# Attention inputs laid out by the host with time along the row, and one scan with its reciprocal in place of two scans

## The chip, the cores and the metric

The kernel runs on one core of a Trainium2 chip. The metric is the device time of one execution in microseconds (us), as the median of several executions. A core has five engines that run side by side, each with its own queue: TensorE (PE in the profile; its weight loads are PEld), VectorE (DVE), ScalarE (ACT), GpSimd (POOL) and SyncE (SP), which here issues most of the transfers. They wait for one another by semaphores. SBUF is the on-chip memory of 128 partitions, PSUM the small memory that TensorE writes to. What the host does with numpy before the launch isn't part of the metric.

## The reference

Two parts follow each other: a linear attention with a decay for every key channel, and a mixture of eight experts of which each token takes one.

```python
batch, n_heads, seq, head_dim = (4, 8, 768, 48)
for t in range(S):
    state = alpha[:, :, t, :, None] * state + einsum('bhd,bhe->bhde', k[:, :, t], v[:, :, t])
    y[:, :, t] = einsum('bhd,bhde->bhe', q[:, :, t], state)
...
x = ascontiguousarray(y.transpose(0, 2, 1, 3)).reshape(B * S, H * D)     # 3072 x 384
logits = x @ w_gate + modality_bias[modality_id]
e_idx = argmax(logits, axis=1)
# probs: softmax of the logits, gate_w: that of the chosen expert
for e in range(8):
    h = maximum(x[mask] @ w1[e], 0.0)               # 384 -> 1024, mask: tokens of e
    out[mask] = gate_w[mask, None] * (h @ w2[e])    # 1024 -> 384
```

All inputs are float32; alpha lies between 0.8 and 1.0.

## The kernel before

**Tiles.** The 3072 tokens are cut into 24 tiles of 128 time steps (NU = 24), six for each batch element. A tile has eight heads of 48 channels; two heads share the 112 partitions of a tile with time along the row: one on partitions 0 to 47, the other on 64 to 111. So a tile of k, q or alpha with time along the row is 112 partitions by 4 pairs by 128 time steps.

**Decays.** Inside a tile the recurrence is turned into matrix products. A key is multiplied by the product of the decays on one side of its time step, a query by that on the other side, and then the scores are plain products of the scaled keys and queries, masked to the past. Before the change, `decay` runs a scan over alpha from the end of the tile to its start (G, L257), which gives each key the decay from its own step to the end. `decay_back` takes the reciprocal of the four whole-tile products (L265) and runs a second scan forward from it (Fw, L267), which gives each query its factor. Rows have segments of 129 columns (SEG): one for each of four pairs, with a column to start the scan anew.

**Inputs.** `load` (L130 to 135) brings alpha, k, q and v with time along the partitions, 48 channels (192 bytes) at a time. TensorE turns alpha, k and q by transposes against an identity matrix (`trans`, L243), four for each, 12 in a step. Alpha is copied from PSUM into X by ScalarE (`decay_in`, L252; in step 0 by VectorE); k and q are read by VectorE from PSUM as they are scaled (`scale_keys`, L283, and `scale`, L291).

**The loop.** L849 to 891 run 24 steps. Step s works on several tiles: the decays of tile s, the scaling, scores and masks of tile s-1, the outputs of tile s-2, the rows of x of tile s-3 (stored to a buffer in DRAM), and the routing of tiles done before. `natural` turns the scaled keys back (L297), `update` forms the tile's own contribution to the state and adds the decayed old one (L354 to 360), `state` and `outputs` form the rows of y (L329, L336). The order on TensorE, VectorE and ScalarE is that in which the code is written (`manual_schedule`, L847), so an instruction that waits holds up all that stand behind it on its engine; GpSimd's work is ordered by a planner. GpSimd masks the scores (L314), keeps the smallest decay product (`amin`, L260) and updates the state (S and T, L358 and L360). `guard` (L270) checks on ScalarE that no alpha is too large; in that case, or where a product got too small, a slow general path runs at the end.

**Routing.** After tiles 5, 11, 15, 19 and 23, `groups` starts the routing of a group: `route_flow` and for two of them `route_early` choose experts and count places, in pieces that `advance` puts into the following steps, with small matrix products on TensorE in between. Behind the loop (L893 to 952) the last tiles, the last routing group and the first expert's work are interleaved by hand. Then the experts run: seven more units of up to 512 tokens.

**Buffers.** Natural-layout tiles of a, k and q have NB = 4 buffers, v has 6; the loads run PF = 3 tiles ahead. PSUM tiles named "tr" (3) take the transposes, "sc" (2) the scores and, before the change, the routing's small products.

Of the kernel before, what the change touches and what calls it, by code (L numbers as in the profile page):

```python
# [21 lines left out]
P = 128  # L22
B, H, S, D = 4, 8, 768, 48
NC = S // P
NP = H // 2
SEG = P + 1
W = 64 + D
SEGS = NP * SEG + 12
DM = H * D
# [34 lines left out]
@with_exitstack  # L64
def attention_moe(ctx: ExitStack, tc: tile.TileContext, q, k, v, alpha, mid, wg, mb, w1, w2, out):
    nc = tc.nc
# [18 lines left out]
    NB, PF, NV = 4, 3, 6  # L85
    nat = {}
    ident = cp.tile([P, P], F32, name="ident")
    make_identity(nc, ident)
    for i in range(NB):
        for n, val in (("a", 1.0), ("k", 0.0), ("q", 0.0)):  # L90
            t = na.tile([P, H, 64], F32, name=f"nat_{n}{i}")
            nat[n, i] = t
            pool.memset(t[:, :, D:], val)

    VT = []
    for i in range(NV):
        t = ac.tile([P, H, 64], F32, name=f"vt{i}")
        VT.append(t)
        pool.memset(t[:, :, D:], 0.0)

# [28 lines left out]

    def load(i, names="akqv"):  # L130
        b, c = divmod(i, NC)
        for n, t in (("a", alpha), ("k", k), ("q", q), ("v", v)):
            if n in names:
                dst = VT[i % NV][:, :, :D] if n == "v" else nat[n, i % NB][:, :, :D]
                sp.dma_start(dst, t[b, :, c * P : (c + 1) * P, :].rearrange("h t d -> t h d"))

    wgs = cp.tile([P, ND, E], F32, name="wgs")
    for n in "a0 k0 q0 a1 v0 a2 k1 q1 v1 a3 k2 q2 v2".split():
        load(int(n[1]), n[0])
    still = ac.tile([P, 4 * P], BF16, name="still")  # L140
# [3 lines left out]
    def warm(n):  # L144
        for _ in range(n):
            pe.matmul(idle, still[:, :P], still, start=True, stop=True)

    warm(7)
    wgp = ac.tile([P, 2, 2, 32], F32, name="wgp")
# [4 lines left out]
    for c in range(2):  # L154
        for g in range(2):
# [3 lines left out]
            )  # L159
    DR = na.tile([W, SEGS], F32, name="DR")[:, : NP * SEG + 1]  # L160
    vec.memset(DR, AFLOOR)
    vec.memset(DR[:, SEG :: SEG], 1.0)
    X, DF, T1 = [], [], []
    for i in range(2):
        t = na.tile([W, SEGS], F32, name=f"X{i}")[:, : NP * SEG + 1]
        vec.memset(t[:, 0 :: SEG], 0.0)
        X.append(t)
        t = na.tile([W, SEGS], F32, name=f"DF{i}")[:, : NP * SEG]
        vec.memset(t, 0.0)
        DF.append(t)  # L170
    for i in range(3):
        t = ac.tile([W, NP, 64], F32, name=f"T1{i}")
        pool.memset(t[:, :, D:], 0.0)
        T1.append(t)
    na.tile([P, 8], F32, name="padr")
    bhi = ac.tile([P, 1], F32, name="bhi")
    vec.memset(bhi, -float(ALPHA_MAX_BITS))
    gacc = ac.tile([P, NU], F32, name="gacc")
    amin = ac.tile([W, NU, NP], F32, name="amin")
    junk = ac.tile([P, DM], F32, name="junk")  # L180
    L = cp.tile([P, NU, E], F32, name="L")
# [57 lines left out]

    def trans(i, n):  # L240
        p = ps.tile([W, NP, P], F32, name="tr", bufs=3)
        for j in range(NP):
            pe.transpose(  # L243
                p[:, j], nat[n, i % NB][:, 2 * j : 2 * j + 2].rearrange("p a b -> p (a b)")[:, :W], ident
            )
        if i == 0 or (i == 1 and n == "a"):
            warm(1)
        return p

    def decay_in(i):  # L250
        pa = trans(i, "a")
        (act.copy if i else vec.tensor_copy)(seg(X[i % 2][:, 1:], 0), pa)  # L252

    def decay(i):
        x = X[i % 2]
        G = na.tile([W, SEGS], F32, name="G", bufs=4)[:, : NP * SEG + 1]
        vec.tensor_tensor_scan(  # L257
            G[:, 1:][:, ::-1], x[:, 1:][:, ::-1], DR[:, 1:][:, ::-1], 0.0, op0=ALU.mult, op1=ALU.max
        )
        pool.tensor_copy(amin[:, i], G[:, 1::SEG])  # L260
        st[i, "G"] = G

    def decay_back(i):
        x, d, G = X[i % 2], DF[i % 2], st[i, "G"]
        vec.reciprocal(d[:, 0::SEG], G[:, 1::SEG])  # L265
        Fw = na.tile([W, SEGS], F32, name="Fw", bufs=3)[:, : NP * SEG]
        vec.tensor_tensor_scan(Fw, x[:, :-1], d, 0.0, op0=ALU.mult, op1=ALU.add)  # L267
        st[i, "F"] = Fw

    def guard(i):  # L270
        return act.activation(
            junk.rearrange("p (a b) -> p a b", b=D),
            nat["a", i % NB][:, :, :D].bitcast(U32),
            AF.Relu,
            bias=bhi,
            scale=1.0,
            accum_out=gacc[:, i : i + 1],
        )

    def scale_keys(i):  # L280
        kh = sb.tile([W, NP, P], F32, name="kh")
        pk = trans(i, "k")
        vec.tensor_tensor(kh, pk, seg(st[i, "G"][:, 1:], 1), op=ALU.mult)  # L283
        st[i, "k"] = kh

    def scale(i):
        if i:
            scale_keys(i)
        qh = sb.tile([W, NP, P], F32, name="qh", bufs=3)
        pq = trans(i, "q")  # L290
        vec.tensor_tensor(qh, pq, seg(st[i, "F"], 1), op=ALU.mult)  # L291
        st[i, "q"] = qh

# [53 lines left out]
    def update(i):  # L347
        if i % NC == NC - 1:
            return
        kn, vt = st[i, "n"], VT[i % NV]  # L350
        kv = ps.tile([W, NP, D], F32, name="kv")
        for h in range(H):
            r = slice(64 * (h % 2), min(64 * (h % 2) + 64, W))
            pe.matmul(kv[r, h // 2], kn[:, h // 2, r], vt[:, h, :D], start=True, stop=True)  # L354
        S1 = sb.tile([W, NP, D], F32, name="S")
        act.copy(S1, kv)
        if i % NC > 0:
            pool.tensor_tensor(S1, S1, T1[i % 3][:, :, :D], op=ALU.add)  # L358
        A = st[i + 1, "G"][:, 1::SEG].unsqueeze(2).broadcast_to([W, NP, D])
        pool.tensor_tensor(T1[(i + 1) % 3][:, :, :D], S1, A, op=ALU.mult)  # L360

# [74 lines left out]
    def route_flow(t0, t1):  # L436
# [16 lines left out]
        yield  # L453
        rp = ps.tile([P, n, E], F32, name="sc", bufs=2)
        pe.matmul(rp, tri, oh[:, s], start=True, stop=False)
# [76 lines left out]
    def route_early(s):  # L532

        n = EARLY[s]
        yield
        cnt = ps.tile([P, E], F32, name="sc", bufs=2)
        pe.matmul(cnt, ones, ohs, start=True, stop=(s == 0))
# [28 lines left out]
        yield  # L566
        tp = ps.tile([P, 2], F32, name="sc", bufs=2)
        for t in range(n):
# [131 lines left out]
    fl = cp.tile([P, 2], F32, name="fl")  # L700
    pool.memset(fl, 1.0)
    flb = cp.tile([P, 1], BF16, name="flb")
    fli = cp.tile([1, 1], I32, name="fli")

    def out_of_range():
        vec.tensor_reduce(fl[:, 0:1], gacc, axis=AX.X, op=ALU.max)
        vec.tensor_reduce(fl[:W, 1:2], amin.rearrange("p a b -> p (a b)"), axis=AX.X, op=ALU.min)
        vec.tensor_scalar(fl[:, 0:1], fl[:, 0:1], 0.0, None, op0=ALU.is_gt)
        vec.tensor_scalar(fl[:, 1:2], fl[:, 1:2], AMIN, None, op0=ALU.is_lt)
        vec.tensor_tensor(flb, fl[:, 0:1], fl[:, 1:2], op=ALU.add)  # L710
        yield
# [102 lines left out]
    def live(i):  # L814
        return 0 <= i < NU
# [33 lines left out]
    for s in range(NU):  # L849
        if s > 0 and s + PF < NU:  # L850
            load(s + PF, "a")
        if s > 0 and s + PF - 1 < NU:
            load(s + PF - 1, "kqv")
# [3 lines left out]
        if s != 1:
            decay_in(s)
        if live(s - 1):
            scale(s - 1)  # L860
        if s == 1:
            decay_in(s)
        if live(s - 3):
            rows(s - 3)
        if live(s - 4) and s % 2:
            logits_rows(s - 4)
        advance()
        if live(s - 1) and (s - 1) % NC < NC - 1:
            natural(s - 1)
        decay(s)  # L870
        if s == 0:
            scale_keys(s)
        if s < NU - 1:
            advance()
# [353 lines left out]


# [20 lines left out]
```

## Time and the profile before

| | us |
|---|---|
| median of three runs | 369.85 (369.78 to 370.48) |
| the profiled execution | 370.23 |
| its span, first to last instruction | 368.5 |
| attention steps, first scan to last scaled query | 6.0 to 137.6 |
| TensorE busy over the span | 356.3 (97%) |
| VectorE busy over the span | 218.3 (59%) |
| ScalarE | 188.1 (51%) |
| GpSimd | 155.6 (42%) |

The page gives a picture of the span in 40 equal slices, each a digit for tenths of busy time:

```profile
PE   8899999999999999999899999999999999999993
DVE  6887879788889875888565415522660456036400
ACT  2766777777767564347454325524451535164310
POOL 9945347426536663047337326313712471220021
PEclk9999999999999999999999999999999999999998
DMA  9999999989899995897756317333633473110011
GB/s 135 166 164 165 178 207 199 195 179 193 171 194 182 199 368 193 297 334 223 254 168 212 101 58 265 101 107 91 232 94 121 134 229 106 65 44 5 1 45 50
```

A slice is 9.2 us, so the attention fills the first 15. PEclk is the clock granted to TensorE, in tenths of the full one; DMA is the busy share of the 16 DMA engines. In the groups further down, a row has the line, engine, operation, what is written and read, the shapes, the count, then busy time in us, the mean duration in ns, and the idle time just before it with what ended it. In a view in order of time, a row begins with the start and the duration in us.

### The profile page before, as it was taken

How to read it: one execution, taken by the hardware profiler on the slowest of the kernel's cores; microseconds unless marked ns; L12 is line 12 of the kernel's file. 1: busy time of each engine (PE TensorE's matmuls, PEld its weight loads, DVE VectorE, ACT ScalarE, POOL GpSimd, SP SyncE). 2: the span in 40 equal slices, each digit the busy share in tenths (PEclk: the TensorE clock that was granted, in tenths of full speed). 3: DMA queues.
4: the chain of work that ended last, by engine and by line, in shares of the span. 5: the costliest groups of instructions: out<-in, count | busy, mean ns of one | idle time of the engine just before them, and what ended most of it. 6: DMA issues, size and time to landing. Idle time of an engine off the chain costs nothing. (4 is left out here: it accounts for less than half of the span.)

```text
span 368.5 us, 9337 instructions
## 1 busy us (share of the span) xinstructions
PE 356.3 (97%) x3666; PEld 314.5 (85%) x3666; DVE 218.3 (59%) x420; ACT 188.1 (51%) x367; POOL 155.6 (42%) x237
## 2 busy tenths in 40 slices
PE   8899999999999999999899999999999999999993
PEld 4788888888988787899888998899899988978992
DVE  6887879788889875888565415522660456036400
ACT  2766777777767564347454325524451535164310
POOL 9945347426536663047337326313712471220021
PEclk9999999999999999999999999999999999999998
DMA  9999999989899995897756317333633473110011
GB/s 135 166 164 165 178 207 199 195 179 193 171 194 182 199 368 193 297 334 223 254 168 212 101 58 265 101 107 91 232 94 121 134 229 106 65 44 5 1 45 50
DMA packets 122730, 59.18 MB, mean 161 GB/s; under 512 B 102857, under 2 KB 114168, under 8 KB 122676
## 3 DMA queue, kind: packets, MB, share of 16 engines
q1 hardware_dynamic: 118196, 48.78, 57.5%
q0 software_dynamic: 4032, 9.68, 7.9%
q8 instruction: 31, 0.51, 0.6%
q14 instruction: 23, 0.19, 0.2%
q10 hardware_dynamic: 448, 0.01, 0.1%
HBM read 49.01 MB, written 9.50 MB: 159 GB/s over the span
## 5 line engine op out<-in xcount | busy, mean ns | idle before, releaser
L965 POOL DMA_INDIRECT out_dram<-os,odx x23 | 23.5, 1020 | 104.4 <-ACT os L1033 93.1
L999 PE MATMUL sc<-w2H,hH 128*128 128x384 f32 x192 | 65.1, 339 | 0.0
L1001 PE MATMUL sc<-w2H,hL 128*128 128x384 f32 x192 | 64.2, 334 | 0.0
L1000 PE MATMUL sc<-w2L,hH 128*128 128x384 f32 x192 | 64.2, 334 | 0.0
L836 DVE TENSOR_TENSOR w1L<-w1r,w1H 128x768 fp32r<-128x768 f32 x24 | 22.0, 955 | 63.1 <-ACT w1H L834 57.7
L1018 PE MATMUL tr<-xH,w1H 128*128 128x512 f32 (+1 forms) x144 | 53.8, 374 | 0.0
L1020 PE MATMUL tr<-xH,w1L 128*128 128x512 f32 (+1 forms) x144 | 53.5, 372 | 0.0
L1019 PE MATMUL tr<-xL,w1H 128*128 128x512 f32 (+1 forms) x144 | 53.5, 371 | 0.0
L828 DVE SCALAR_TENSOR_TENSOR hL<-tr,hH 128x512 fp32r<-128x512 f32 x47 | 32.3, 688 | 32.8 <-ACT hH L826 25.6
L826 ACT ACTIVATE hH<-tr 128x512 fp32r<-128x512 f32 x47 | 28.0, 598 | 44.9 <-PE tr L1020 24.5
L314 POOL TENSOR_SCALAR_AFFINE_SELECT scT<-scT 128x512 f32<-128x512 f32 x48 | 38.0, 815 | 21.5 <-ACT scT L313 21.5
L1033 ACT ACTIVATE os<-sc,gg 128x384 f32<-128x384 f32 x23 | 13.4, 582 | 64.8 <-PE sc L1001 37.3
L696 POOL DMA_INDIRECT gg<-gd,idx x25 | 26.9, 1076 | 25.8 <-DMA gd<-gs 18.8
L999 PEld LDWEIGHTS sc<-w2H,hH 128*128 128x128 f32 x192 | 36.1, 188 | 1.1 <-issue 1.0
L1000 PEld LDWEIGHTS sc<-w2L,hH 128*128 128x128 f32 x192 | 36.1, 188 | 0.1
L1001 PEld LDWEIGHTS sc<-w2H,hL 128*128 128x128 f32 x192 | 36.0, 188 | 0.0
L313 ACT COPY scT<-sc 128x512 f32<-128x512 f32 x48 | 25.8, 589 | 14.5 <-PE sc L309 14.4
L267 DVE TENSOR_TENSOR_SCAN Fw<-X,DF 112x516 f32<-112x516 f32 x24 | 32.0, 1335 | 0.8
L690 POOL DMA_INDIRECT xg<-xd,idx x25 | 26.6, 1063 | 11.5 <-issue 4.9
L1020 PEld LDWEIGHTS tr<-xH,w1L 128*128 128x128 f32 x144 | 27.1, 188 | 4.7
L1018 PEld LDWEIGHTS tr<-xH,w1H 128*128 128x128 f32 x144 | 27.1, 188 | 4.6
L1019 PEld LDWEIGHTS tr<-xL,w1H 128*128 128x128 f32 x144 | 27.1, 188 | 4.6
(245 smaller groups left out, 672.9 us busy)
## 6 DMA issues: line engine op xcount, KB each, us to landing
w1r<-in_moe_w_dram SPq DMA_DIRECT2D x16, 768.0 KB
w2r<-in_moe_w_dram SPq DMA_DIRECT2D x16, 768.0 KB
nat_a<-in_alpha_dram SPq DMA_DIRECT2D x24, 192.0 KB
nat_k<-in_k_dram SPq DMA_DIRECT2D x24, 192.0 KB
nat_q<-in_q_dram SPq DMA_DIRECT2D x24, 192.0 KB
vt<-in_v_dram SPq DMA_DIRECT2D x24, 192.0 KB
xd<-xs SPq DMA_DIRECT2D x24, 192.0 KB
xg<-xd,idx POOLq DMA_INDIRECT x25
```

The source lines that it names most:

```text
L267: vec.tensor_tensor_scan(Fw, x[:, :-1], d, 0.0, op0=ALU.mult, op1=ALU.add)
L314: pool.affine_select(s, s, [[0, NP], [1, P]], ALU.is_ge, 0.0, base=0, channel_multiplier=-1)
L690: pool.indirect_dma_start(xg[x][:, u], None, xd[0:rows], IOA(idx[:, c : c + 1], 0), bounds_check=rows - 1, oob_is_err=False)
L696: pool.indirect_dma_start(gg[x][:, u : u + 1], None, gd[0:rows], IOA(idx[:, c : c + 1], 0), bounds_check=rows - 1, oob_is_err=False)
L826: act.activation(hH, hp, AF.Relu)
L828: vec.scalar_tensor_tensor(hL, hp, 0.0, hH.bitcast(F32), op0=ALU.max, op1=ALU.subtract)
L999: pe.matmul(op, hH[:, us] if f is None else hH[:, f, us], wH, start=first, stop=False)
L1000: pe.matmul(op, hH[:, us] if f is None else hH[:, f, us], wL, start=False, stop=False)
L1001: pe.matmul(op, hL[:, us] if f is None else hL[:, f, us], wH, start=False, stop=final)
L1018: pe.matmul(hp, wH[:, d, fs], XH[:, d, :n], start=(d == 0), stop=False)
L1019: pe.matmul(hp, wH[:, d, fs], XL[:, d, :n], start=False, stop=False)
L1020: pe.matmul(hp, wL[:, d, fs], XH[:, d, :n], start=False, stop=(d == ND - 1))
```

## The change

The host lays out two new inputs. `turned` holds for each of the 24 tiles 112 partitions by 1552 columns: keys (512), queries (512), and alpha in four segments of 129, each behind a column with 0 (ones and zeros fill partitions 48 to 63). `rowsv` holds v with time along the partitions, each head padded to 64 columns. The general path still reads q, k, v and alpha as they are.

On the chip the transposes of alpha, k and q go, with X, DF and the copy into X. One forward scan G gives the product of the decays since the tile's start, restarted by the 0 and a 1.0 in DR at the head of each segment; R is the reciprocal of all 516 columns of G. Keys are multiplied by R, queries by G; the state's decay is G's last column of the same tile. `scale(s)` runs in step s, after the first `advance`, no longer in step s+1, and `groups` stands behind it. The guard reads alpha in the new layout. The routing's small products use the PSUM tiles "tr" in the loop and "sc" behind it. The first four loads bring all 112 partitions, later ones the 96 with data. Four more warm-up products of TensorE stand at the start.

```diff
+AW = NP * SEG + 12
+KW = NP * P
+RW = 2 * KW + AW
...
+    TN = [na.tile([W, RW], F32, name=f"tn{i}") for i in range(NB)]
...
+    def load(i, v=True):
+        if i >= NB:
+            for r in (slice(0, D), slice(64, W)):
+                sp.dma_start(TN[i % NB][r], turned[i, r])
+        elif i:
+            sp.dma_start(TN[i], turned[i])
+        else:
+            for c in (slice(2 * KW, RW), slice(0, KW), slice(KW, 2 * KW)):
+                sp.dma_start(TN[0][:, c], turned[0, :, c])
+        sp.dma_start(VT[i % NV], rowsv[i])
...
-    warm(7)
+    warm(11)
...
+    DR = na.tile([W, AW], F32, name="DR")[:, : NP * SEG]
     vec.memset(DR, AFLOOR)
+    vec.memset(DR[:, 0::SEG], 1.0)
...
     def decay(i):
-        x = X[i % 2]
...
-    def decay_back(i):
...
+        G = na.tile([W, AW], F32, name="G", bufs=3)[:, : NP * SEG]
+        vec.tensor_tensor_scan(G, TN[i % NB][:, 2 * KW : 2 * KW + NP * SEG], DR, 0.0, op0=ALU.mult, op1=ALU.max)
+        pool.tensor_copy(amin[:, i], G[:, P::SEG])
+        R = na.tile([W, AW], F32, name="R", bufs=2)[:, : NP * SEG]
+        vec.reciprocal(R, G)
+        st[i, "G"], st[i, "R"] = G, R
...
     def scale(i):
+        for n, z, f in (("k", 0, "R"), ("q", 1, "G")):
+            t = sb.tile([W, NP, P], F32, name=n + "h", bufs=3)
+            src = TN[i % NB][:, z * KW : (z + 1) * KW].rearrange("p (a b) -> p a b", b=P)
+            vec.tensor_tensor(t, src, seg(st[i, f], 1), op=ALU.mult)
+            st[i, n] = t
...
-        A = st[i + 1, "G"][:, 1::SEG].unsqueeze(2).broadcast_to([W, NP, D])
+        A = st[i, "G"][:, P::SEG].unsqueeze(2).broadcast_to([W, NP, D])
...
-        rp = ps.tile([P, n, E], F32, name="sc", bufs=2)
+        rp = ps.tile([P, n, E], F32, **place)
...
     for s in range(NU):
+        if s + PF < NU:
+            load(s + PF)
...
+        decay(s)
+        if live(s - 1) and (s - 1) % NC < NC - 1:
+            natural(s - 1)
         if live(s - 3):
             rows(s - 3)
         if live(s - 4) and s % 2:
             logits_rows(s - 4)
         advance()
-        if live(s - 1) and (s - 1) % NC < NC - 1:
-            natural(s - 1)
-        decay(s)
-        if s == 0:
-            scale_keys(s)
+        scale(s)
         if s < NU - 1:
             advance()
         if s % 2:
             groups(s - 4)
-        decay_back(s)
-        guard(s)
...
+        guard(s)
         if live(s - 2):
             state(s - 2)
         if live(s - 1):
             scores(s - 1)
...
     L0 = NU - 1
-    scale(L0)
+    place.update(name="sc", bufs=2)
     rows(L0 - 2)
```

More of the change, by code (lines that the diff above doesn't have):

```diff
@@ L27 @@
 W = 64 + D
-SEGS = NP * SEG + 12
+AW = NP * SEG + 12
+KW = NP * P
+RW = 2 * KW + AW
 DM = H * D
@@ L64, in attention_moe @@
 @with_exitstack
-def attention_moe(ctx: ExitStack, tc: tile.TileContext, q, k, v, alpha, mid, wg, mb, w1, w2, out):
+def attention_moe(ctx: ExitStack, tc: tile.TileContext, q, k, v, alpha, mid, wg, mb, w1, w2, turned, rowsv, out):
     nc = tc.nc
@@ L85, in attention_moe @@
     NB, PF, NV = 4, 3, 6
-    nat = {}
     ident = cp.tile([P, P], F32, name="ident")
     make_identity(nc, ident)
[L89 to L93, printed above, removed]
+    TN = [na.tile([W, RW], F32, name=f"tn{i}") for i in range(NB)]
     VT = []
@@ L98, in attention_moe @@
         VT.append(t)
-        pool.memset(t[:, :, D:], 0.0)
     WR = [
@@ L128, in first_unit @@
             )
[L130 to L135, printed above, removed]
+    def load(i, v=True):
[8 more added lines that the diff above has]
+        sp.dma_start(VT[i % NV], rowsv[i])
     wgs = cp.tile([P, ND, E], F32, name="wgs")
-    for n in "a0 k0 q0 a1 v0 a2 k1 q1 v1 a3 k2 q2 v2".split():
-        load(int(n[1]), n[0])
+    for i in range(PF):
+        load(i)
     still = ac.tile([P, 4 * P], BF16, name="still")
@@ L159, in attention_moe @@
             )
-    DR = na.tile([W, SEGS], F32, name="DR")[:, : NP * SEG + 1]
+    DR = na.tile([W, AW], F32, name="DR")[:, : NP * SEG]
     vec.memset(DR, AFLOOR)
[L162 to L170, printed above, removed]
+    vec.memset(DR[:, 0::SEG], 1.0)
+    na.tile([P, 8], F32, name="padr")
+    T1 = []
     for i in range(3):
@@ L174, in attention_moe @@
         T1.append(t)
-    na.tile([P, 8], F32, name="padr")
     bhi = ac.tile([P, 1], F32, name="bhi")
     vec.memset(bhi, -float(ALPHA_MAX_BITS))
-    gacc = ac.tile([P, NU], F32, name="gacc")
+    gacc = ac.tile([W, NU], F32, name="gacc")
     amin = ac.tile([W, NU, NP], F32, name="amin")
-    junk = ac.tile([P, DM], F32, name="junk")
+    junk = ac.tile([W, NP * SEG], F32, name="junk")
     L = cp.tile([P, NU, E], F32, name="L")
@@ L238, in seg @@
         return t.rearrange("p (a b) -> p a b", b=SEG)[:, :, lo : lo + P]
[L240 to L252, printed above, removed]
-    def decay(i):
-        x = X[i % 2]
[L256 to L261, printed above, removed]
-    def decay_back(i):
[L264 to L268, printed above, removed]
+    def decay(i):
+        G = na.tile([W, AW], F32, name="G", bufs=3)[:, : NP * SEG]
[4 more added lines that the diff above has]
+        st[i, "G"], st[i, "R"] = G, R
     def guard(i):
         return act.activation(
-            junk.rearrange("p (a b) -> p a b", b=D),
-            nat["a", i % NB][:, :, :D].bitcast(U32),
+            junk,
+            TN[i % NB][:, 2 * KW : 2 * KW + NP * SEG].bitcast(U32),
             AF.Relu,
-            bias=bhi,
+            bias=bhi[:W],
             scale=1.0,
@@ L278, in guard @@
         )
[L280 to L284, printed above, removed]
-    def scale(i):
[L287 to L292, printed above, removed]
+    def scale(i):
+        for n, z, f in (("k", 0, "R"), ("q", 1, "G")):
[3 more added lines that the diff above has]
+            st[i, n] = t
     def natural(i):
@@ L427, in attention_moe @@
     odx = cp.tile([P, NH], I32, name="odx")
+    place = {"name": "tr", "bufs": 3}
     def route_begin():
@@ L535, in route_early @@
         yield
-        cnt = ps.tile([P, E], F32, name="sc", bufs=2)
+        cnt = ps.tile([P, E], F32, **place)
         pe.matmul(cnt, ones, ohs, start=True, stop=(s == 0))
@@ L566, in route_early @@
         yield
-        tp = ps.tile([P, 2], F32, name="sc", bufs=2)
+        tp = ps.tile([P, 2], F32, **place)
         for t in range(n):
@@ L700, in attention_moe @@
     fl = cp.tile([P, 2], F32, name="fl")
-    pool.memset(fl, 1.0)
+    pool.memset(fl[:, 0:1], 0.0)
+    pool.memset(fl[:, 1:2], 1.0)
     flb = cp.tile([P, 1], BF16, name="flb")
@@ L705, in out_of_range @@
     def out_of_range():
-        vec.tensor_reduce(fl[:, 0:1], gacc, axis=AX.X, op=ALU.max)
+        vec.tensor_reduce(fl[:W, 0:1], gacc, axis=AX.X, op=ALU.max)
         vec.tensor_reduce(fl[:W, 1:2], amin.rearrange("p a b -> p (a b)"), axis=AX.X, op=ALU.min)
@@ L849, in attention_moe @@
     for s in range(NU):
[L850 to L853, printed above, removed]
+        if s + PF < NU:
+            load(s + PF)
         if s == 4:
@@ L856, in attention_moe @@
             sp.dma_start(gd[MID : MID + 1], zr[:, 0:1])
[L857 to L862, printed above, removed]
+        decay(s)
+        if live(s - 1) and (s - 1) % NC < NC - 1:
+            natural(s - 1)
         if live(s - 3):
@@ L1227, with laid_out @@
 _OUTS = [((N, DM), "float32")]
+def laid_out(np, q, k, v, alpha):
+    turned = np.zeros((NU, W, RW), np.float32)
+    for z, x in enumerate((k, q)):
+        x = x.reshape(B, NP, 2, NC, P, D).transpose(0, 3, 2, 5, 1, 4).reshape(NU, 2, D, KW)
+        turned[:, :D, z * KW : (z + 1) * KW] = x[:, 0]
+        turned[:, 64:, z * KW : (z + 1) * KW] = x[:, 1]
+    a = np.ones((NU, W, NP, SEG), np.float32)
+    x = alpha.reshape(B, NP, 2, NC, P, D).transpose(0, 3, 2, 5, 1, 4).reshape(NU, 2, D, NP, P)
+    a[:, :D, :, 1:], a[:, 64:, :, 1:] = x[:, 0], x[:, 1]
+    a[:, :, :, 0] = 0.0
+    turned[:, :, 2 * KW : 2 * KW + NP * SEG] = a.reshape(NU, W, NP * SEG)
+    rowsv = np.zeros((NU, P, H, 64), np.float32)
+    rowsv[..., :D] = v.reshape(B, H, NC, P, D).transpose(0, 2, 3, 1, 4).reshape(NU, P, H, D)
+    return {"turned": turned, "rowsv": rowsv}
 def kernel(**inputs):
@@ L1238 @@
     arrays, args = {}, []
-    for name in _INS:
-        a = _np.ascontiguousarray(inputs[name])
+    given = {name: _np.ascontiguousarray(inputs[name]) for name in _INS}
+    given.update(laid_out(_np, *(given[n] for n in ("q", "k", "v", "alpha"))))
+    for name, a in given.items():
         arrays[f"in_{name}_dram"] = a
```

## The prediction

> **What bounds the kernel now.** I read the page's busy shares first, then busy times by stage, then the groups by line on VectorE, then one step in order of time. Up to about 137 us the kernel runs the 24 steps of the attention; after that the experts run. The change touches only the first part, so what it is worth is read there.
>
> ```profile
> 6.00:137.60 131.60, 128.59 (x2308) 111.25 (x2310) 110.21 (x206) 91.56 (x212) 72.15 (x132) 1.00 1.07 196
> 69.78:74.89 5.11, 5.11 (x91) 4.48 (x86) 3.98 (x8) 3.60 (x9) 1.45 (x3) 1.00 1.17 196
> ```
>
> Columns: window, its length, busy us of PE, PEld, DVE, ACT, POOL, granted clock, DMA share, GB/s. A step lasts 131.6 / 24 = 5.48 us on average; a plain one, from one scan of VectorE to the next, 5.11. In it TensorE is busy all the time, VectorE for 4.0 us. VectorE is second: 110.2 of 131.6 us.
>
> ```profile
> L267 DVE TENSOR_TENSOR_SCAN Fw<-X,DF 112x516 f32<-112x516 f32 x24 | 32.0, 1335 | 0.8
> L257 DVE TENSOR_TENSOR_SCAN G<-X,DR 112x516 f32<-112x516 f32 x24 | 29.7, 1240 | 0.0
> L283 DVE TENSOR_TENSOR kh<-tr,G 112x512 f32<-112x512 f32 x24 | 16.5, 689 | 18.6 <-PE tr L243 18.2
> L291 DVE TENSOR_TENSOR qh<-tr,Fw 112x512 f32<-112x512 f32 x24 | 16.3, 681 | 0.2
> L265 DVE RECIPROCAL DF<-G 112x4 f32<-112x4 f32 x24 | 4.3, 177 | 0.4
> ```
>
> These groups are VectorE's between 6.0 and 137.6 us. Its only long wait is that of kh for the transposes on TensorE (18.2 us in all); in steps with routing work there is little of it, and VectorE itself sets the pace. So **TensorE leads, with VectorE 21 us behind** over the whole part.
>
> ```profile
> 73.55 0.69 DVE L283 TENSOR_TENSOR kh<-tr,G 112x512 f32<-112x512 f32 x1 [1.06 <-PE tr L243]
> 74.16 0.68 DVE L291 TENSOR_TENSOR qh<-tr,Fw 112x512 f32<-112x512 f32 x1
> 74.75 0.21 DVE L389 TENSOR_REDUCE L<-kv 128x16 f32<-128x64 f32 x1
> 74.89 1.22 DVE L257 TENSOR_TENSOR_SCAN G<-X,DR 112x516 f32<-112x516 f32 x1
> 76.14 0.18 DVE L265 RECIPROCAL DF<-G 112x4 f32<-112x4 f32 x1
> ```
>
> The order of time gives the pitches, start to start: scan 1.25, kh 0.61, qh 0.60 us.
>
> **The change part by part.** *TensorE.* The three groups of transposes (L243) go:
>
> ```profile
> 55.98 0.65 PE L243 MATMUL tr<-ident,nat_a 128*112 128x128 f32 x4
> ...
> 57.34 0.62 PE L367 MATMUL tr<-ident,yt 128*128 128x128 f32 x4
> ```
>
> From alpha's, the first, to the start of what follows q's, the last, is 1.36 us, 24 times 32.6 us. A step's TensorE work falls from 5.11 (5.48 on average) to 3.75 (4.12) us. If TensorE still led, that would be the gain.
>
> *VectorE.* The second scan (1335 ns) and the reciprocal of 4 elements (177 ns) go: 1.51 us. A reciprocal of 516 elements comes in. The trace has none; it has three small ones, L265 above and these:
>
> ```profile
> L676 DVE RECIPROCAL gt<-sm 128x20 f32<-128x20 f32 x1 | 0.3, 278 | 0.0
> ...
> L676 DVE RECIPROCAL gt<-sm 128x4 f32<-128x4 f32 x1 | 0.2, 177 | 0.0
> ```
>
> Sixteen more elements cost 101 ns: 6.3 ns each, where kh does an element in some 1.0 to 1.3 ns (689 ns for 512). Carried on to 516 elements: 0.278 + 496 x 0.0063 = **3.41 us**. The lower bound is the rate of kh, 0.7 us. For an upper one I take as the instruction's fixed part the shortest operation at hand, and give all else to the elements:
>
> ```profile
> 120.17 0.13 DVE L546 TENSOR_REDUCE base<-rest 128x1 f32<-128x8 f32 x1
> ```
>
> (278 - 130) / 20 = 7.4 ns, and 0.13 + 516 x 0.0074 = 3.95 us. I take 3.41: all three reciprocals lie on its line (fixed part 152 ns), and both on L676 have one form. Net on VectorE: 3.41 - 1.51 = +1.90 us a step, **+45.6 us** in 24 steps, against 18.2 us of waiting that it can swallow.
>
> The Trainium skill ("VectorE: DVE Perf Modes", First, the fixed hardware budget) says that the reciprocal is an iterative divide with a repeat count of 8. It speaks against the change; at its 0.96 GHz, 516 elements would be an estimated 4.3 us, and the total about 21 us above mine. The rows agree in kind but give 6.3 ns, not 8.3, and so the sum goes by the rows.
>
> *kh and qh* now read both inputs from SBUF, not one from PSUM. The nearest row of that kind:
>
> ```profile
> L836 DVE TENSOR_TENSOR w1L<-w1r,w1H 128x768 fp32r<-128x768 f32 x24 | 22.0, 955 | 63.1 <-ACT w1H L834 57.7
> ```
>
> 256 elements more than kh for 266 ns more: the same rate, no difference (bound: 0.05 us either way). But such operations block GpSimd:
>
> ```profile
> 11.65 1.25 DVE L267 TENSOR_TENSOR_SCAN Fw<-X,DF 112x516 f32<-112x516 f32 x1
> 11.93 0.96 POOL L260 COPY amin<-G 112x4 f32<-112x4 f32 x1
> ...
> 54.27 0.19 POOL L260 COPY amin<-G 112x4 f32<-112x4 f32 x1 [1.92 <-DVE G L257]
> ...
> 55.34 2.17 POOL L314 TENSOR_SCALAR_AFFINE_SELECT scT<-scT 128x512 f32<-128x512 f32 x2 [0.89 <-ACT scT L313]
> 55.42 0.17 DVE L265 RECIPROCAL DF<-G 112x4 f32<-112x4 f32 x1
> 55.63 1.45 DVE L267 TENSOR_TENSOR_SCAN Fw<-X,DF 112x516 f32<-112x516 f32 x1
> ```
>
> A copy of 0.19 us takes 0.96 and ends with the scan; a scan that starts within a select takes 1.45 instead of 1.23. The reciprocal at 55.42, started within the same select, isn't stretched. The Trainium skill ("SBUF — State Buffer", Who interferes with whom) has the same: two SBUF inputs contend with a GpSimd instruction that reads SBUF. So kh and qh can now each wait for one of GpSimd's operations (the masks, S, T: up to about 0.6 us), while most masks should fall under the long reciprocal. From nothing to 0.65 us a step; I take 0.2, as in the scans above, **+4.8 us**.
>
> *The start.* The first scan needed a transfer, transposes and a copy:
>
> ```profile
> 2.97 0.06 DVE L162 MEMSET DR<- 112x4 f32 x1
> ...
> 4.22 1.07 PE L243 MATMUL tr<-ident,nat_a 128*112 128x128 f32 x4
> 5.33 0.69 DVE L252 COPY X<-tr 112x512 f32<-112x512 f32 x1 [2.30 <-PE tr L243]
> 6.05 1.23 DVE L257 TENSOR_TENSOR_SCAN G<-X,DR 112x516 f32<-112x516 f32 x1
> ```
>
> Now it starts when alpha has landed: between 3.0 (the memsets) and 4.4 us (as now, with 237 instead of 197 KB at 196 GB/s). I take 3.7: **-2.3 us**.
>
> *Transfers.* A step loads 596 + 262 = 858 KB in place of 786, in rows of up to 6.2 KB in place of 192 bytes. Even at the present 196 GB/s that is 4.4 us, under a step of 6 us or more; it costs nothing either way. It would show only if steps fell under 4.4 us. SyncE's queue has three loads and a store a step as against four and one.
>
> *ScalarE* loses X's copy and gets a longer guard; with 91.6 / 24 = 3.8 us busy in a step it stays under VectorE, at no cost.
>
> *The end.* scale(23) now stands ahead of groups(19), so the six routing operations of tiles 16 to 19 come behind the last qh (-1.2 us from the chain up to it), while TensorE, in its written order, meets their result before the scores of tile 23:
>
> ```profile
> 133.39 0.17 DVE L447 TENSOR_TENSOR L<-L,bt 128x32 f32<-128x32 f32 x1
> ...
> 134.59 0.17 DVE L265 RECIPROCAL DF<-G 112x4 f32<-112x4 f32 x1
> ...
> 136.84 0.67 DVE L291 TENSOR_TENSOR qh<-tr,Fw 112x512 f32<-112x512 f32 x1
> ...
> 137.87 1.05 PE L309 MATMUL sc<-qh,kh 48*64 48x128 f32 x32
> ```
>
> Now the scores start 0.3 us after qh has ended. Then they wait for those operations (1.2), the rank products, a half-step of logits and the state products (about 1 us together): **+2 us** (0 to 4).
>
> **Sum.** The last qh ends at 137.5 us (VectorE's path of 131.6 without the waiting is 113.4). Less 18.2 of waiting, plus 45.6, less 1.2, plus 4.8, less 2.3: 166.2 us, 28.7 later. With 2 at the end +30.7. What follows is bound by TensorE and keeps its length. The profiled execution took 370.2 us, so 400.9; the median of the runs is 0.4 lower: **400.5 us**. The 32.6 us taken off TensorE are lost: it will idle about 2 us in a step.
>
> **The rivals.** *(a) The long reciprocal is cheap per element* (faster). At 0.7 us VectorE has 1.25 + 0.7 + 1.21 = 3.2 us a step, and beside it what its present path has over (113.4 - 24 x (1.51 + 1.25 + 1.21) = 18): 94 us; TensorE leads with 24 x 4.12 = 99; from 3.7 us on, with some waits, the part ends near 105 instead of 137.5, total about 338. It decides below the point where 24 x (r - 1.51) covers what is left of 18.2 + 1.2 - 4.8 + 2.3 - 2 = 14.9 us, so below r = 2.1 us. The 20-element row speaks against it: at kh's rate it would be 0.19, not 0.28 us. *(b) The reciprocal or the blocking is dearer*: 3.95 us gives +13, so 413; blocking at 0.65 us adds 11 more. *(c) The reciprocal keeps GpSimd out too*: then GpSimd's work, up to 72.15 / 24 = 3.0 us a step, fits nowhere beside VectorE's: up to +72, about 465. The 55.42 row speaks against it. *(d) TensorE's clock falls*, since it idles in each step: at half the clock 4.12 us become 8.2, against some 6.8 (162.5 / 24) in my sum: +35, about 435. The granted clock is 1.00 in all windows here and shows nothing of it. *(e) About nothing*, r near 2.1: no row gives that.
>
> **How the numbers follow.** Forecast (388 to 410) 0.67; (b) 0.16; (a) 0.09; (c) 0.03; (d) 0.03; (e) 0.02. Within the forecast: blocking from nothing (-4.8) up, the end from 0 to 4, the start 0.7 either way give 393 to 409; a fixed part that hides some of the slope gives the rest. The range 388 to 420 leaves out (a), (c), (d), (e) and the far end of (b), about 0.2. Faster by over 0.2% (what a measurement of this kernel can tell from no change): (a) and half of (e), 0.10; slower: 0.88.
>
> **What would show it.** The reciprocal's group: 24 of 112x516 at about 3.4 us, 82 us in all. VectorE over 95% busy in the steps, and steps of 5.9 us without routing. TensorE waits for kh and qh; nothing waits for transfers. A reciprocal under 2.1 us proves me wrong in sign, kh and qh over 0.9 us on average in the blocking.

## The result and the profile after

| | before | after |
|---|---|---|
| median of four runs, us | 369.81 (368.20 to 370.48) | 402.78 (398.29 to 403.49) |
| ratio, 95% interval | | 1.087 (1.079 to 1.096) |
| the profiled execution / its span, us | 370.23 / 368.5 | 403.49 / 401.8 |
| first scan starts | 6.05 | 3.94 |
| last qh ends | 137.51 | 162.93 |
| scores of tile 23 start | 137.87 | 166.58 |
| first product of the experts with w2 (L999, then L955) | 157.31 | 188.55 |

The kernel became 33 us slower; 400.5 had been forecast, in a range from 388 to 420. Here and below, executions over 1.5% above the fastest of their kernel count in the medians and ranges, but not in the ratios. Of the 33.3 us between the two spans 25.4 arose up to the last qh, 5.8 from there to the first w2 product, and 2.1 in the experts' part.

The page of the kernel after, some of the pictures in 40 slices, each now 10.0 us:

```profile
PE   4488596967668767799979999999999999999992
...
DVE  6699999999999999559683650653355156116400
```

TensorE and VectorE have changed places: from the third to the 16th slice DVE stands at 9, and PE, which stood at 9 before, at 4 to 9. Engine busy times by stage (window, length, PE, PEld, DVE, ACT, POOL, granted clock, DMA share, GB/s) for the steps and the seam behind the loop:

```profile
3.94:162.93 158.99, 113.82 (x2007) 90.62 (x2004) 152.94 (x175) 83.49 (x188) 55.77 (x126) 0.88 0.76 179
165.00:170.00 5.00, 5.00 (x73) 4.10 (x72) 1.53 (x8) 1.45 (x3) 0.73 (x2) 0.53 0.00 0
```

VectorE is busy for 152.94 of 158.99 us, 96%; it was 84% before. The groups by line on VectorE up to 163 us say with what:

```profile
L237 DVE RECIPROCAL R<-G 112x516 f32<-112x516 f32 x24 | 81.1, 3378 | 0.8
L234 DVE TENSOR_TENSOR_SCAN G<-tn,DR 112x516 f32<-112x516 f32 x24 | 29.4, 1226 | 5.6 <-DMA tn<-in_turned_dram 5.4 <-issue 0.3
L254 DVE TENSOR_TENSOR kh<-tn,R 112x512 f32<-112x512 f32 x24 | 17.3, 719 | 0.5
L254 DVE TENSOR_TENSOR qh<-tn,G 112x512 f32<-112x512 f32 x24 | 16.8, 701 | 0.0
```

The reciprocal alone takes 81.1 us, over half of the part. The wait of kh for TensorE (18.2 us before) is gone. One step in order of time shows that VectorE has no gap left:

```profile
83.82 1.22 DVE L234 TENSOR_TENSOR_SCAN G<-tn,DR 112x516 f32<-112x516 f32 x1
85.08 3.38 DVE L237 RECIPROCAL R<-G 112x516 f32<-112x516 f32 x1
88.49 1.03 DVE L254 TENSOR_TENSOR kh<-tn,R 112x512 f32<-112x512 f32 x1
89.44 0.68 DVE L254 TENSOR_TENSOR qh<-tn,G 112x512 f32<-112x512 f32 x1
90.05 1.22 DVE L234 TENSOR_TENSOR_SCAN G<-tn,DR 112x516 f32<-112x516 f32 x1
```

6.23 us from scan to scan, against 5.11 in the step shown of before; this kh is one of the few that were held up (1.03 instead of 0.69 us). And the waits (engine, line, for whom, us in total, times, longest) show who waits for VectorE now, and one thing that wasn't expected, the last row:

```profile
PE tr L260 <- DVE kh L254: 21.8, 12, 5.4
...
DVE G L234 <- DMA tn<-in_turned_dram: 5.4, 2, 3.4
```

### The profile page after: what moved, and what is told of

Read it like the earlier page. It is cut to its first block, busy times and chain, and to the rows that moved or that the text cites. A ratio compares the mean times of both kernels' runs of the same rounds, so it can differ in the third digit from the quotient of the medians.

```text
span 401.8 us, 8565 instructions
## 1 busy us (share of the span) xinstructions
PE 343.7 (86%) x3378; PEld 295.8 (74%) x3378; DVE 261.4 (65%) x391; ACT 179.5 (45%) x344; POOL 138.6 (35%) x220
## 5 line engine op out<-in xcount | busy, mean ns | idle before, releaser
L237 DVE RECIPROCAL R<-G 112x516 f32<-112x516 f32 x24 | 81.1, 3378 | 0.8
L955 PE MATMUL sc<-w2H,hH 128*128 128x384 f32 x192 | 65.1, 339 | 0.0
L955 PEld LDWEIGHTS sc<-w2H,hH 128*128 128x128 f32 x192 | 36.1, 188 | 1.1 <-issue 1.0
L235 POOL COPY amin<-G 112x4 f32<-112x4 f32 x24 | 4.5, 187 | 91.7 <-DVE G L234 91.7
L277 POOL TENSOR_SCALAR_AFFINE_SELECT scT<-scT 128x512 f32<-128x512 f32 x48 | 30.1, 649 | 11.1 <-ACT scT L276 11.1
L272 PE MATMUL sc<-qh,kh 48*64 48x128 f32 x768 | 30.7, 304 | 3.5 <-DVE mt L213 3.5
L299 PE MATMUL y<-scT,vt 128*64 128x128 f32 x384 | 31.6, 307 | 2.1 <-POOL scT L277 1.1
L234 DVE TENSOR_TENSOR_SCAN G<-tn,DR 112x516 f32<-112x516 f32 x24 | 29.4, 1226 | 5.6 <-DMA tn<-in_turned_dram 5.4
```

Source lines behind the costliest of these rows:

```text
L234: vec.tensor_tensor_scan(G, TN[i % NB][:, 2 * KW : 2 * KW + NP * SEG], DR, 0.0, op0=ALU.mult, op1=ALU.max)
L237: vec.reciprocal(R, G)
L272: pe.matmul(pp[g][z, j], kh[r, j, z], qh[r, j], start=True, stop=True)
L277: pool.affine_select(s, s, [[0, NP], [1, P]], ALU.is_ge, 0.0, base=0, channel_multiplier=-1)
L299: pe.matmul(y[z, g, h * P : (h + 1) * P], vt[:, 2 * j + g], sc[g][:, j], start=(i % NC == 0 and h == 0), stop=(h == 1),)
L955: pe.matmul(op, hH[:, us] if f is None else hH[:, f, us], wH, start=first, stop=False)
```

## The experiments

Four theories. **1**: the reciprocal's length sets the pace, and without it the change would gain what it takes off TensorE. **2**: the new layout, the order or TensorE's lower clock costs the time, and the reciprocal only fills the gaps. **3**: kh and qh with both inputs in SBUF and GpSimd's operations hold one another up, and with a short reciprocal this is what decides. **4**: it is the order of the work and the first loads. Theories 3 and 4 were formed after the first kernels. The median of before beside these runs was 369.89, 370.71 or 371.78 us (three chips); ratios are to that of the same chip.

**The new layout with both scans.** The reciprocal goes back to 4 elements, everything else stays as changed.

```diff
-        vec.reciprocal(R, G)
+        vec.reciprocal(d[:, 0::SEG], G[:, 1::SEG])
+        vec.tensor_tensor_scan(Fw, x[:, :-1], d, 0.0, op0=ALU.mult, op1=ALU.add)
...
-        for n, z, f in (("k", 0, "R"), ("q", 1, "G")):
+        for n, z, f in (("k", 0, st[i, "G"][:, 1:]), ("q", 1, st[i, "F"])):
```

(G is scanned from the end again, as before.)

> The changed kernel with one part undone: the two scans and the 4-element reciprocal are back, the host's layout stays. Theory 1 (the 516-element reciprocal on VectorE sets the pace): a step loses 3.38 us and gets 1.23 + 0.18 back, 24 times 1.95 = 47 us off VectorE's path, so 352 to 360 us, faster than before too, since no transpose is waited for. Theory 2 (the layout, the new order in the step or TensorE's lower clock makes it slow): the time stays at 385 or more.

Measured: 389.93 us (385.47 to 395.29), ratio 1.053 (1.047 to 1.059). That is some 13 us less than after, 30 more than the top of theory 1's range, and within theory 2's 385 or more: **theory 1 alone falls**. TensorE was relieved of its 32.6 us here too, and VectorE of the long reciprocal, and still the kernel is slower than before. Of the 15.2 us between the span of its profiled execution (383.7) and that of before, 9.4 arise up to the last qh (146.92) and 5.3 from there to the first w2 product (25.1 in place of 19.8). VectorE's groups in the profile of this run:

```profile
L244 DVE TENSOR_TENSOR_SCAN Fw<-tn,DF 112x516 f32<-112x516 f32 x24 | 38.4, 1598 | 0.8
L238 DVE TENSOR_TENSOR_SCAN G<-tn,DR 112x516 f32<-112x516 f32 x24 | 30.3, 1262 | 5.0 <-DMA tn<-in_turned_dram 4.9
L261 DVE TENSOR_TENSOR kh<-tn,G 112x512 f32<-112x512 f32 x24 | 24.4, 1019 | 0.0
L261 DVE TENSOR_TENSOR qh<-tn,Fw 112x512 f32<-112x512 f32 x24 | 20.6, 860 | 1.1 <-DMA tn<-in_turned_dram 1.1
```

kh takes 1019 ns and the second scan 1598, where before had 689 and 1335. The same elements, the same operations: something holds them up. From this came theory 3.

**The reciprocal in the old layout.** Before's transposes and order, with one scan and the long reciprocal.

```diff
+        vec.tensor_tensor_scan(G, x[:, :-1], DR, 0.0, op0=ALU.mult, op1=ALU.max)
+        vec.reciprocal(R, G)
...
-        vec.tensor_tensor(kh, pk, seg(st[i, "G"][:, 1:], 1), op=ALU.mult)
+        vec.tensor_tensor(kh, pk, seg(st[i, "R"], 1), op=ALU.mult)
```

> The kernel before with the other part alone: one forward scan and the 516-element reciprocal, with all transposes and the old loads. Theory 1: VectorE's path is 113.4 + 24 x 1.87 = 158 us, longer than TensorE's 132, so 392 to 400 us, although nothing of TensorE's work has gone. Theory 2: TensorE keeps busy with its transposes, its clock stays up, and the time is near that of before, under 380 us.

Measured: 398.25 us (396.18 to 399.48), ratio 1.075 (1.069 to 1.081). The long reciprocal in place of the second scan, without any of the layout, costs 28 us. Its group and the steps by stage:

```profile
L260 DVE RECIPROCAL R<-G 112x516 f32<-112x516 f32 x24 | 81.1, 3378 | 0.8
```

```profile
6.03:163.77 157.74, 134.72 (x2310) 113.26 (x2312) 153.55 (x181) 91.54 (x212) 58.46 (x132) 0.98 0.88 168
```

3378 ns to the nanosecond as in after, VectorE busy for 153.55 of 157.74 us, and the last qh at 163.77 where after has 162.93. TensorE has 20.9 us more to do in this part than after, at a clock of 0.98 instead of 0.88, and the time is the same: beside the long reciprocal the removed transposes are worth nothing.

**TensorE kept busy.** Eight products of 512 columns that nobody reads stand in each step behind `update`, so that the clock stays up.

```diff
+        fill = ps.tile([P, 4 * P], F32, name="tr", bufs=3)
+        for _ in range(8):
+            pe.matmul(fill, still[:, :P], still, start=True, stop=True)
```

> The changed kernel with eight dummy matmuls (128x512 bf16, result not used) behind the update of every step, some 1.7 us of TensorE's idle time. Theory 1: VectorE's path up to the last scaled query is unchanged within 2 us; the granted clock is near 1.00, and only what stands behind the loop gets shorter: 396 to 401 us. Theory 2 (the clock costs the loop its time): under 390 us, with the last scaled query 8 us earlier or more.

Measured: 399.34 us (397.68 to 401.11), ratio 1.080 (1.075 to 1.085). The last qh ends at 162.04, 0.9 us earlier than in after, and the second scan, which waits for the first loads, had started 1.2 us earlier (12.21 for 13.38). The clock isn't what bounds the loop. It does cost something behind it: between 165 and 170 us after was granted 0.53, this kernel 1.00,

```profile
165.00:170.00 5.00, 5.00 (x94) 4.01 (x83) 2.56 (x15) 2.90 (x6) 1.22 (x2) 1.00 0.12 43
```

and from the last qh to the first w2 product it needs 22.1 us, where after needs 25.6 and before 19.8.

**The routing ahead of the scaling in the last step.** So the small operations of tiles 16 to 19 don't stand behind the last qh.

```diff
         advance()
+        if s == NU - 1:
+            groups(s - 4)
         scale(s)
...
-        if s % 2:
+        if s % 2 and s < NU - 1:
             groups(s - 4)
```

> The changed kernel with one move: in the last step the routing group of tiles 16 to 19 is started ahead of scale, as before the change. Theory of the end (TensorE meets the group's rank products ahead of the scores of tile 23 and waits): the scores start 0.5 us behind the last scaled query in place of 3.7, the query ends 1.2 us later, 2 us off in all: 399 to 402 us. Rival (the end is longer for TensorE's clock or the gather): no difference within 1 us.

Measured: 398.26 us (396.75 to 402.23), ratio 1.076 (1.068 to 1.085). Order of time at the seam, VectorE and TensorE:

```profile
162.32 1.08 DVE L254 TENSOR_TENSOR qh<-tn,G 112x512 f32<-112x512 f32 x1
...
163.46 1.20 PE L272 MATMUL sc<-qh,kh 48*64 48x128 f32 x32
```

The scores start 0.06 us after the last qh, and the w2 products 19.6 us after it, as before (19.8). So the order at the seam, with the clock that it brings about, accounts for the whole 5.8 us there. Not all of it is gained: the qh ends 0.5 us later than in after although the second scan started 1.2 us earlier (12.14 for 13.38), so about 1.7 us more stand ahead of it, where 1.2 had been written (the last qh itself took 1.08 us for 0.68). The medians differ by 4.5 us, and the ranges overlap. The reading is in after's own TensorE, in order of time:

```profile
164.72 0.19 PE L420 MATMUL sc<-oh,tri 128*128 128x32 bf16 x1 [1.72 <-DVE oh L417]
...
166.58 1.93 PE L272 MATMUL sc<-qh,kh 48*64 48x128 f32 x32
```

TensorE waits 1.72 us for VectorE's routing, does what stands ahead of the scores, and then runs the scores at a granted clock of 0.50 (166.58 to 168.51 us): 1.93 us, 1.05 before.

**The loads of the first three tiles split**, on top of the kernel just above, with tile 1 ahead of the values of tile 0.

```diff
-    for i in range(PF):
-        load(i)
+    cols(0, ca, ck, cq)
+    cols(1, ca, ck, cq)
+    sp.dma_start(VT[0], rowsv[0])
+    cols(2, ca)
+    sp.dma_start(VT[1], rowsv[1])
+    cols(2, ck, cq)
+    sp.dma_start(VT[2], rowsv[2])
```

> routing_ahead_of_scale with the first loads reordered: tile 1 in three parts ahead of the first v, so that the second scan needn't wait for the 695 KB of tile 1 behind v. If the second scan's 3.4 us of waiting counts in full (VectorE sets the pace from there on), 3 to 4 us less than routing_ahead_of_scale: about 394.5 us. If the transfers as a whole are too slow at the start (some 200 GB/s), a later scan waits instead and less than 1.5 us is gained.

Measured: 395.77 us (394.73 to 396.75), ratio 1.066 (1.059 to 1.073), 2.5 less than without the edit; the last qh ends 2.5 us earlier as well (160.91 for 163.40). That falls between what was written; the intervals of the two ratios overlap, and it is the traces that carry the reading. VectorE's second scan in after and, second, here:

```profile
13.38 1.23 DVE L234 TENSOR_TENSOR_SCAN G<-tn,DR 112x516 f32<-112x516 f32 x1 [3.43 <-DMA tn<-in_turned_dram]
```

```profile
9.86 1.22 DVE L244 TENSOR_TENSOR_SCAN G<-tn,DR 112x516 f32<-112x516 f32 x1
```

The wait for tile 1 is gone. In the kernel without the split the second scan started at 12.14, so 2.3 us lay there, and all of it reaches the last qh: the first loads were on the path.

**Alpha alone turned by the host.** Before, with its two scans and its order, k and q still turned by TensorE into PSUM.

```diff
+    TA = [na.tile([W, SEGS], F32, name=f"ta{i}") for i in range(NB)]
...
+                sp.dma_start(TA[i % NB], alphat[i])
...
-    def decay_in(i):
-        pa = trans(i, "a")
-        (act.copy if i else vec.tensor_copy)(seg(X[i % 2][:, 1:], 0), pa)
...
-        x = X[i % 2]
+        x = TA[i % NB][:, : NP * SEG + 1]
```

> The kernel before with alpha alone laid out by the host (no transposes of alpha, no copy into X); k and q are still transposed on TensorE and read from PSUM, both scans stay. Against two_scans_new_layout it has eight transposes a step more on TensorE, but kh and qh read only one input from SBUF. Theory 3 (with two SBUF inputs, kh and qh block GpSimd and wait for it, and the late masks hold up TensorE): scan Fw back to about 1.34, kh and qh to 0.69 us, the masks to about 0.8 us, TensorE's work 5.48 - 0.45 = 5.03 us a step, last scaled query at 124 to 131 us, 356 to 364 us in all, faster than before. Theory 4 (two_scans_new_layout is slow for its order, its loads or TensorE's idle time): no better than the kernel before.

> alpha_only_two_scans unaltered, beside it on the same chip: 361 to 365 us.

Measured: 363.49 us (361.00 to 363.95), ratio 0.977 (0.969 to 0.984), and on another chip 363.74 (362.47 to 364.65), ratio 0.977 (0.973 to 0.982). **This version is faster than both kernels**: both intervals lie below 1. The last qh ends at 131.96 and 129.22 us. GpSimd's masks take 890 and 892 ns, where some 0.8 us had been written. VectorE's groups in the second of the runs:

```profile
L263 DVE TENSOR_TENSOR_SCAN Fw<-ta,DF 112x516 f32<-112x516 f32 x24 | 32.4, 1349 | 0.8
L253 DVE TENSOR_TENSOR_SCAN G<-ta,DR 112x516 f32<-112x516 f32 x24 | 30.8, 1282 | 0.8 <-DMA ta<-in_alphat_dram 0.8
L287 DVE TENSOR_TENSOR qh<-tr,Fw 112x512 f32<-112x512 f32 x24 | 16.3, 678 | 0.1
L279 DVE TENSOR_TENSOR kh<-tr,G 112x512 f32<-112x512 f32 x24 | 16.2, 676 | 12.6 <-PE tr L243 12.6
```

kh and qh read PSUM and take 676 and 678 ns. kh still waits 12.6 us for the transposes: TensorE has less to do, and still leads.

**Both scans, new layout, and before's order.** To part theory 3 from the order: the first kernel of this section with `scale(s-1)` again at the head of step s, `decay_back` and `guard` behind `groups`, the loads one step later, and the routing's products in "sc".

```diff
-        decay(s)
-        if live(s - 1) and (s - 1) % NC < NC - 1:
-            natural(s - 1)
+        if live(s - 1):
+            scale(s - 1)
...
-        scale(s)
+        if live(s - 1) and (s - 1) % NC < NC - 1:
+            natural(s - 1)
+        decay(s)
...
+        decay_back(s)
+        guard(s)
```

> two_scans_new_layout (k, q and alpha from the host's layout, both scans) with the order of the step as in the kernel before: tile s-1 scaled at the start of step s, the second scan behind the routing, routing in PSUM tiles sc, the end as before. Against alpha_only_two_scans it differs in k and q alone: read from SBUF, no transposes of them. Theory 3 (two SBUF inputs block GpSimd and wait for it): kh and qh over 0.8 us on average, GpSimd's masks or T over those of alpha_only_two_scans, and slower than it by 5 us or more although TensorE has 0.9 us less to do in each step: 368 to 385 us. Rival (the new order of the step was at fault): 350 to 362 us, kh and qh near 0.69 us.

Measured: 380.54 us (378.96 to 382.74), ratio 1.021 (1.016 to 1.027). The order that would have given 350 to 362 is not the cause. Against the alpha-only kernel this one also takes k's and q's transposes off TensorE, and it is 16.8 us slower. VectorE's groups, and then GpSimd's:

```profile
L248 DVE TENSOR_TENSOR_SCAN Fw<-tn,DF 112x516 f32<-112x516 f32 x24 | 34.0, 1418 | 0.8
L238 DVE TENSOR_TENSOR_SCAN G<-tn,DR 112x516 f32<-112x516 f32 x24 | 31.3, 1306 | 4.0 <-DMA tn<-in_turned_dram 4.0
L265 DVE TENSOR_TENSOR qh<-tn,Fw 112x512 f32<-112x512 f32 x24 | 25.1, 1048 | 1.1 <-DMA tn<-in_turned_dram 1.1
L265 DVE TENSOR_TENSOR kh<-tn,G 112x512 f32<-112x512 f32 x24 | 23.0, 958 | 0.0
```

```profile
L334 POOL TENSOR_TENSOR T<-S,G 112x192 f32<-112x192 f32 x20 | 17.8, 888 | 1.3
L332 POOL TENSOR_TENSOR S<-S,T 112x192 f32<-112x192 f32 x16 | 14.6, 911 | 0.4 <-ACT S L330 0.2
```

The same two GpSimd groups of the alpha-only kernel:

```profile
L354 POOL TENSOR_TENSOR S<-S,T 112x192 f32<-112x192 f32 x16 | 10.3, 643 | 0.8 <-POOL scT L310 0.5
L356 POOL TENSOR_TENSOR T<-S,G 112x192 f32<-112x192 f32 x20 | 10.3, 513 | 1.3
```

The four VectorE operations of a step are 1418 + 1306 + 958 + 1048 = 4730 ns here and 1349 + 1282 + 676 + 678 = 3985 there: 745 ns, in 24 steps 17.9 us; the last qh ends 17.4 us later (146.66 for 129.22). What VectorE waits is much the same in both, but for other things: there 12.6 us for the transposes, here 6.1 for small products of the routing and 5.1 for the first loads. On GpSimd T goes from 513 to 888 ns and S from 643 to 911. The masks are long in both (914 and 892).

Single operations of the same run show what stretches them. VectorE and GpSimd in order of time, two steps:

```profile
19.78 0.67 DVE L265 TENSOR_TENSOR kh<-tn,G 112x512 f32<-112x512 f32 x1
20.36 0.68 DVE L265 TENSOR_TENSOR qh<-tn,Fw 112x512 f32<-112x512 f32 x1
...
22.25 0.19 POOL L241 COPY amin<-G 112x4 f32<-112x4 f32 x1 [3.62 <-DVE G L238]
22.39 2.15 POOL L288 TENSOR_SCALAR_AFFINE_SELECT scT<-scT 128x512 f32<-128x512 f32 x2
...
24.03 1.05 DVE L265 TENSOR_TENSOR kh<-tn,G 112x512 f32<-112x512 f32 x1
25.00 0.68 DVE L265 TENSOR_TENSOR qh<-tn,Fw 112x512 f32<-112x512 f32 x1
```

The first pair runs while GpSimd is idle. The second kh starts beside a mask and takes 1.05 us, and its qh, behind the mask, 0.68 again. In the whole run 5 kh and 8 qh run with nothing of GpSimd beside them, none over 0.69 us; of the 19 kh and 16 qh beside one of its operations, 16 and 15 take 0.93 us or more. In the alpha-only kernel all 24 kh and 20 of 24 qh run beside GpSimd too, and none takes over 0.70 us. **So kh and qh stretch where they read both inputs from SBUF and GpSimd works beside them**: theory 3 holds. A run with GpSimd's work moved away from beside them was not made.

**The reciprocal on ScalarE**, as Ln and Exp, on top of the kernel with the routing ahead.

```diff
-        vec.reciprocal(R, G)
+        act.activation(ln, G, AF.Ln)
+        act.activation(R, ln, AF.Exp, scale=-1.0)
```

> routing_ahead_of_scale with R formed on ScalarE as exp(-ln G), two activations of 112x516 in place of the 3.38 us on VectorE; everything else is kept, kh and qh with two SBUF inputs too. Theory 1 alone: VectorE's path loses 81 us, less some waiting of kh for ScalarE (about 1.5 us a step), so 350 to 365 us, unless table loads of 1.28 us stand between the two functions. Theory 3: with the long reciprocal gone, GpSimd's masks collide with G, kh and qh (kh or qh over 0.85 us on average, masks over 0.9 us): 370 to 390 us.

Measured, in two runs: 414.68 us (413.92 to 415.44), ratio 1.117 (1.107 to 1.126). Neither range: the exception that theory 1 had named, table loads between the two functions, came true. ScalarE's groups:

```profile
L238 ACT ACT_TABLE_LOAD x24 | 30.8, 1283 | 4.4 <-DMA tn<-in_turned_dram 4.0
L239 ACT ACT_TABLE_LOAD x24 | 30.8, 1283 | 0.4
L238 ACT ACTIVATE lnG<-G 112x516 f32<-112x516 f32 x24 | 15.2, 633 | 4.1 <-DVE G L234 3.8
L239 ACT ACTIVATE R<-lnG 112x516 f32<-112x516 f32 x24 | 15.2, 633 | 0.3
```

Two table loads a step cost 61.6 us, twice the arithmetic, and ScalarE, busy for 163.9 of 169.4 us, took over as the bound. VectorE waited for R (71.6 us in all), so that only two kh and two qh of 24 each came beside an operation of GpSimd. They took 693 and 686 ns on average: two inputs in SBUF alone don't stretch them. The collision that theory 3 expected here didn't come about.

**After again**, unaltered, on the chip of the second group of runs:

> The changed kernel unaltered, on the same chip as the three others: 398 to 403 us; the reciprocal at 3.38 us.

Measured: 403.69 us (398.67 to 404.92), just above what was written; the reciprocal took 3378 ns. The last qh ends at 162.46 and the w2 products start 24.1 us later: what is said of after doesn't hang on one execution.

## Why the prediction held, point by point

- **The bound.** TensorE led, VectorE was the next, and swapped they are: DVE 96% busy in the steps. A step without routing lasts 5.89 us (from the scan at 13.38 to that at 19.27), 5.9 had been written.
- **The price of the reciprocal**, the term that set the sign. 3.41 us from two small reciprocals, measured 3.378: in 24 steps 0.8 us less. From 20 to 516 elements it rises by (3378 - 278) / 496 = 6.25 ns each. The old layout with the reciprocal in place of the second scan shows the cost without anything else: +28 us. The repeat count of 8 in the Trainium skill ("VectorE: DVE Perf Modes", First, the fixed hardware budget), read as eight cycles an element, had given an estimated 4.3 us; the runs don't show that.
- **TensorE's gain is lost.** True: PE is busy for 114 of 159 us, and with 20.9 us more of work in the old layout the last qh ends at the same time.
- **The blocking of kh and qh** was mis-sized here, 0.2 us a step against (719 - 689 + 701 - 681) = 0.05, so 3.6 us too much in all. GpSimd's masks run beside the long reciprocal and are short there. Before, and then after:

```profile
L314 POOL TENSOR_SCALAR_AFFINE_SELECT scT<-scT 128x512 f32<-128x512 f32 x46 | 36.8, 823 | 19.7 <-ACT scT L313 19.7
L277 POOL TENSOR_SCALAR_AFFINE_SELECT scT<-scT 128x512 f32<-128x512 f32 x46 | 28.9, 650 | 6.0 <-ACT scT L276 6.0
```

  "Most masks should fall under the long reciprocal" was right, and should have lowered the term. What hid it is the reciprocal itself: without that, kh and qh of the same layout pay 958 + 1048 - 676 - 678 = 652 ns a step, the upper bound that was written, and the two scans another 93.
- **Transfers "cost nothing either way": this step failed.** It looked at the steady state, 858 KB a step, and there nothing waits. But tile 1 now lands whole: 695 KB of tile 0, 262 of its values and 695 of tile 1 are 1.65 MB ahead of the second scan. Up to that scan, at 13.38 us, 186 GB/s moved 2.5 MB, since the values of tile 1 and tile 2, issued from 4.64 us on, were under way as well:

```profile
0.00:13.38 13.38, 8.20 (x63) 4.61 (x63) 6.93 (x10) 2.63 (x4) 6.61 (x38) 0.81 0.83 186
```

  VectorE is ready at 9.95 us. The wait is 3.4 us (2.3 to 2.4 in three other executions with these loads), and splitting the loads removes it.
- **The start**: 3.94 instead of 3.7; **the rest of the loop** came out 2.5 us shorter than the sum. About 1.9 of it are VectorE's operations other than those named: 11.4 us before, 8.3 after, of which 1.2 had moved behind the last qh. Why they got shorter was not followed up. Together -3.6 - 0.8 + 3.4 + 0.2 - 2.5 = -3.3: the last qh at 162.93 instead of 166.2.
- **The end** was named, with its cause, and sized at +2 of 0 to 4; it is +5.8, in the second execution +4.3. The step that failed counted VectorE's six operations and the products that move ahead of the scores, and left out TensorE's clock. With the clock held up by the products that nobody reads, this stretch is 22.1 us, 2.3 over before and close to the +2. The other 3.5 us (2.0 in the second execution) go with the clock, 0.53 between 165 and 170 us in the one and 0.70 in the other.
- **The experts' part** was to keep its length. It takes 213.25 us and before 211.19, with the same busy times (TensorE 203.25 and 203.21); where the 2.1 us lie stays open. In the two profiled executions of the alpha-only kernel this part takes 210.4 and 213.2 us, so 2.1 is no more than one kernel varies by.

So -3.3 + 3.8 + 2.1 = +2.6 us turn the forecast span of 399.2 into 401.8: errors of both signs, which by chance nearly cancel.

Of the rivals, (a) fell with the measured reciprocal; but its price of 338 us looks wrong too, since it kept kh and qh at their old length. With two short operations in place of the long one the same layout took 390 and, in before's order, 381 us; a kernel with a short reciprocal was not at hand. Rival (c) is contradicted by the masks at 650 ns; its price, by its own terms 400.5 + 72, should have been about 472 us, not 465. Rival (d) was half right: the clock falls (0.88 on average in the steps), but 114 us of TensorE's work at that clock still fit beside VectorE's 153; it shows only behind the loop.

## What to carry to other kernels

Price an operation that comes in by the slope over its elements, from whatever sizes of it the trace has, and not by the rate of its neighbours: two reciprocals of 4 and 20 elements gave that of 516 within 1%. When inputs move from PSUM to SBUF, look at what GpSimd does beside the operation that reads them; each of kh and qh went from 0.68 to about 1 us on average though nothing of their arithmetic changed. And when a change has several parts, time each alone: here alpha's layout by itself was worth 2.3%, while the long reciprocal in place of the second scan took 7.5%, and the layout of k and q, with its longer first loads, about 4.6% (380.54 against 363.74) where its blocking had no cover.

## What the runs showed of the hardware that was not expected

- The reciprocal of 112x516 f32 took 3378 ns on average in every kernel that has it, all 24 in after beside some operation of GpSimd and none over 3379. It doesn't keep GpSimd out (masks at 650 ns), and GpSimd doesn't stretch it.
- A kh or qh with both inputs in SBUF took 0.66 to 0.69 us with GpSimd idle and mostly 0.93 to 1.1, at most 2.8, beside one of its operations; with one input in PSUM it took 0.66 to 0.69 either way.
- The clock granted to TensorE fell to 0.53 (165 to 170 us) after idle gaps of 2.21, 1.60 and 1.72 us in the 11 us before, none longer, and in a second execution of the same kernel to 0.70 in that window. The Trainium skill ("TensorE: Matmul & The Clock Gate", What's actually happening) puts the fall behind an idle window of about 3.4 us; here shorter gaps in close succession had already been enough. Between 95 and 105 us, at 84% busy, the grant was 1.00.
- With all DMA engines busy (share 1.03) the loads between 10 and 20 us, in rows of 2 and 6.2 KB, moved 224 GB/s; between 158 and 161 us the engines moved 375 at a share of 1.05. Why is not shown.
- Ln followed by Exp loaded a table each time, 1283 ns, 48 times in 24 steps.
